# A gate ahead of GpSimd's first load, a re-planned order, and a last tile of 384 and 128 columns

## The chip, the core and the metric

The kernel runs on one core of a Trainium2 chip. Its engines have queues of their own: TensorE (PE, with PEld for weight loads), VectorE (DVE), ScalarE (ACT), GpSimd (POOL) and SyncE (SP, which here only issues DMAs). The metric is the time of one execution in device microseconds: 287.45 us, the median of three runs (285.32 to 287.76).

## What is computed

A linear attention over 8 batches, 8 heads, 576 tokens and 64 channels, and an FFN with a maximum over three products:

```python
def phi(x):
    proj = np.einsum('bhsd,df->bhsf', x, w_phi)
    proj = proj - np.max(np.abs(proj), axis=-1, keepdims=True)
    return np.concatenate([np.exp(proj), np.exp(-proj)], axis=-1)
...
kv = np.einsum('bhsf,bhsd->bhfd', phi(k), v)
num = np.einsum('bhsf,bhfd->bhsd', phi(q), kv)
den = np.einsum('bhsf,bhf->bhs', phi(q), z)[..., None] + 1e-06
...
h = np.maximum(np.maximum(x @ w1, x @ w2), x @ w3)
return h @ w_out
```

z is the sum of phi(k) over the tokens; x is num / den with the heads of a token side by side (4608 x 512); w1 to w3 are 512 x 768, w_out is 768 x 512.

## The kernel before

The attention is cut into 16 units of four heads (two units a batch), the FFN into nine chunks of 512 tokens: eight of 512 of a batch's 576 tokens, and a last one of the eight batches' remaining 64.

A unit goes through these steps. Its q, k and v are loaded. q and k become bf16 (qk_bf) and are turned by PE (tps) or by a DMA transpose into qkT. PE projects them (psq, psk). DVE takes the largest absolute values (mqp for q, mk for k), ACT makes the exponentials Ek of k. The maxima of k become a factor em, and GpSimd multiplies v with it into vab (line 589) and copies em beside it (line 599). PE projects q a second time with the maxima taken off (psm), ACT makes Eq from it. PE multiplies Ek and vab into kv (kvps, line 643, 72 matmuls), then Eq and kv (psn), DVE divides, and the result is turned into xT.

How q and k come in differs by unit. Unit 0's q and k come in two halves each, four loads on SP's queue (line 447), and ACT casts them. Units 1 to 3 are loaded by GpSimd's queue with a cast on the way (line 458). Later units come as float32, and GpSimd casts them (line 476). v comes as float32 by SP or GpSimd (line 472). For some v loads a DVE copy of one element into the target (line 467) makes the load wait until some unit's qkT is there; this is called a gate.

The four weights come through GpSimd's queue (w_load, line 419): w1, w2 and w3 into w_bf, w_out into wout_bf. h is computed as x w1 + max(0, x (w2 - w1), x (w3 - w1)), so GpSimd subtracts w1 from the second and third weight (line 785), three pieces each, before the FFN's first products (ups, line 714), and a product w1 w_out is made once: w1 is turned by PE (pwT) and multiplied (pm, line 811). A chunk's output tile is xT times this product (ops, line 742) plus the maximum times w_out (line 747); it is copied to SBUF (line 755) and stored (line 762).

The order of all this is written out by hand: PLAN lists every step as number, engine, buffers and a start time, and plan() hands the steps to their engines in this order. The start times aren't waited for on the chip; what waits is each engine, in its own order, for the data and buffers of its next instruction. DVE's queue begins with memsets and three casts of w_phi (lines 405 and 406), whose two halves ACT's queue loads. fill() puts matmuls of constants (idlers, line 842) where PLAN leaves PE a gap.

The last output tile is made in two pieces of 256 columns, so that the first piece's copy and store lie beside the second piece's matmuls.

Of the kernel before, what the change touches and what calls it, by code (L numbers as in the profile page):

```python
# [95 lines left out]
0G@0.7 4A@0.7 6S0@0.7 2D0@0.8 3D@1.0 10S0@1.2 1G@1.3 12S@1.6 85G0@1.9 8S@2.1 84G@2.6 1075G@3.3 158G1@4.0 5D@4.1  # L96
157G@4.7 7A2@5.0 14G0@5.5 1078G@6.2 11A@6.3 1076G@6.9 15T1@7.2 13A@7.3 361G1@7.7 16D0@7.8 360G1@8.4 21T002300@8.6
26T45@8.8 24D@9.0 9A@9.1 29D@9.6 28A@9.7 19T6@10.0 17T7@10.2 27A@10.2 20D@10.4 22A@10.7 227G2@10.7 41T1@10.7 18D@10.8
23A@11.1 226G@11.4 30D@11.4 31T24@11.5 36T67@11.8 32A@12.0 34D@12.0 90T5@12.1 33A@12.4 39D@12.6 88T2@12.7 38A@12.9
44D@13.2 37A@13.4 89D1@13.5 54T60@13.9 43A@13.9 40D@14.1 92T2@14.4 55A@14.5 86D1@14.7 93D@14.8 63T7@14.9 87S@14.9  # L100
25D@15.0 56A@15.0 114T11211@15.3 947S2@15.3 42A@15.5 35D@15.6 60T6@15.6 64A@15.7 1085T3@16.1 91D@16.2 65A@16.2
99T40@16.6 62A@16.7 45D@16.8 57T7@17.0 117D@17.1 61A@17.2 1089T5@17.4 159D3@17.4 102D@17.5 59A@17.6 104T16@17.9
1090D0@18.1 58A@18.1 163T4@18.3 46A0@18.6 118D@18.7 94T75@18.8 50A@18.9 164D2@19.0 115A@19.2 53G0@19.3 47G@19.5
116A@19.5 1086D@19.6 95A@19.7 165T4@19.8 66T2@20.0 96A@20.2 107D@20.2 48G@20.6 67A@20.7 166D@20.8 68A@21.0 109T31@21.0
97D@21.0 100A@21.2 1087T4@21.3 112D@21.6 51G@21.7 101A@21.7 161T2@21.8 106A@22.2 1088D@22.2 139T71@22.6 49A@22.7
52G@22.8 105A@22.8 130T3@22.8 98D@22.8 127T4@23.2 141A@23.3 103D@23.4 140A@23.5 131A@23.8 160G@23.9 69T057@24.0
162D@24.0 119A1@24.3 111A@24.5 120G1@24.7 129A@25.0 228D0@25.4 108D@25.4 121G@25.8 133T0@26.1 71D@26.2 70A@26.2
# [12 lines left out]
1111T0@45.7 257A@45.8 249D@45.9 1082G@45.9 201A@46.1 250D@46.5 258A@46.6 261T5@46.8 253A@46.9 202T2@46.9 262D1@47.1  # L120
366T004700@47.2 1112D@47.2 264A1@47.3 263S@47.3 214T056@47.5 1110A@47.6 369D@47.8 1083G@48.0 204A@48.1 229S@48.2
203A@48.6 381T01@48.6 426S1@48.6 216D@48.8 1123T4@48.9 248A@49.0 215D@49.2 384D@49.5 368A@49.5 211T2@49.8 386T6@49.9
385D@50.1 213A@50.1 299G1@50.1 1115T5@50.1 212A@50.4 367A@50.6 1124D@50.7 1107T0@51.0 382A@51.1 267G1@51.2 389D@51.3
556S0@51.3 298G@51.4 247A@51.6 370D@51.6 268T21@51.9 208T4@52.1 1108D@52.2 270A@52.3 1119T3@52.3 300S2@52.6 269A@52.7
1116D@52.8 1121T7@53.2 388A@53.2 265G@53.3 387A@53.5 209A@53.8 390D@53.9 371T02@54.1 210A@54.2 1120D@54.2 277T5@54.4
1117T6@54.6 383A@54.7 374D@54.8 278A@55.2 266G@55.3 1122D@55.4 280T4@55.5 271T3@55.6 279A@55.7 223T10@55.8 1118D@56.0
281A@56.1 274T0@56.1 555S0@56.2 1113T7@56.4 282A@56.4 224D0@56.6 273A@56.7 362S3@56.7 276A@57.2 376T56@57.3 559G2@57.4
283T141@57.6 272A@57.6 379D@57.7 275A@58.1 375D@58.3 428G0@58.5 391T3@58.8 1125T5@58.8 1114D@58.9 392A0@59.0 377A@59.2
393S@59.3 284D@59.5 429G@59.6 378A@59.6 1129T0@59.7 285D@59.9 491S0@60.1 373A@60.1 380D@60.3 372A@60.6 306T113711@60.7
430S1@60.8 316T41@60.9 310D@61.1 321T6@61.2 317A@61.3 221T2@61.4 309D@61.7 1130T@61.7 323A@61.8 319D@62.3 325D@62.9  # L130
219T3@63.0 320D@63.2 1131A0@63.2 217T4@63.3 1126T@63.6 394A0@63.7 222D1@63.8 318A@64.0 396G0@64.1 220D0@64.4 307A@64.4
# [160 lines left out]
def kernel(  # L292
# [133 lines left out]
    def attention(u):  # L426
# [4 lines left out]
        def nd(kind, *args, **kw):  # L431
            return node(kind, u, *args, **kw)
# [441 lines left out]
```

## Time and profile before

| | |
|---|---|
| median of three runs | 287.45 us |
| the profiled execution | 286.68 us |
| its span, from the first to the last instruction | 284.9 us |
| PE / DVE / ACT / POOL busy | 273.7 / 207.9 / 192.4 / 124.4 us |
| granted TensorE clock, mean | 0.998 |
| read from HBM / written | 34.67 / 9.44 MB |

The page's shares are averages over the span. The head (about the first 40 us) brings in the weights and the first units, the middle mixes units and FFN chunks, and the tail is FFN alone. In timelines a row gives start, length, engine, line, operation and tile; a bracket tells how long the engine stood idle ahead of it and what ended that. A DMA row on an engine is the issue alone; when its data land is told by the DMA view.

### The profile page before, as it was taken

What the parts mean: (1) busy time and instruction counts of PE and PEld (TensorE: products, weight loads), DVE (VectorE), ACT (ScalarE), POOL (GpSimd) and SP (SyncE); (2) the same over time, 40 slices, a digit from 0 to 9 for tenths busy, and PEclk for the clock granted to TensorE, in tenths of its full rate; (3) what the DMA queues carried; (4) which work ended last, traced back from release to release, by engine and by line L of the source; (5) the groups of instructions that cost most, each with busy time, mean ns of one, the idle gap of its engine ahead of it and who ended that gap; (6) DMA issues with size and microseconds to landing.
All of it is one profiled execution on the core that took longest, in us unless ns stands there. A gap on an engine that the chain in (4) does not pass through costs nothing.

```text
span 284.9 us, 8444 instructions
## 1 busy us (share of the span) xinstructions
PE 273.7 (96%) x3485; PEld 155.3 (55%) x3523; DVE 207.9 (73%) x442; ACT 192.4 (68%) x448; POOL 124.4 (44%) x104
## 2 busy tenths in 40 slices
PE   8789999989999999999999999999999999999995
PEld 3466674455665656556465565555544664444443
DVE  2799899989889886898678779987875462227431
ACT  3799779988899899967768887779775500041001
POOL 9359997786387543670554760160080601000000
PEclk9999999999999999999999999999999999999999
DMA  6999999999999979898995989293420035153126
GB/s 194 205 283 258 321 195 237 354 262 240 220 281 298 214 157 321 206 199 223 230 264 213 267 191 188 100 182 81 83 65 3 21 41 110 35 112 76 37 77 182
DMA packets 67760, 51.46 MB, mean 181 GB/s; under 512 B 48778, under 2 KB 53002, under 8 KB 67722
## 3 DMA queue, kind: packets, MB, share of 16 engines
q1 hardware_dynamic: 62761, 43.45, 62.6%
q0 software_dynamic: 4576, 7.28, 12.4%
q8 instruction: 27, 0.44, 0.6%
q10 hardware_dynamic: 385, 0.21, 0.3%
q14 instruction: 11, 0.09, 0.1%
HBM read 34.67 MB, written 9.44 MB: 155 GB/s over the span
## 4 chain that ended last, share of the span: by engine, by line
PE 76%; DMA 9%; DVE 6%; ACT 4%; issue 2%; POOL 1%; SPq 1%; ACTq 0%; POOLq 0%
PE ups L714 28%; PE ops L747 15%; PE ops L742 10%; PE psn L661 6%; PE kvps L643 6%; PE psm L614 4%; PE psq L535 4%; DMA q_raw<-in_q_dram 3%; ACT Ek L548 2%; DMA qkT<-mT 2%; DMA v_raw<-in_v_dram 2%; DVE mqp L554 2%; DMA xT<-x_sb 2%; DVE mk L554 2%; DVE hT L720 1%
## 5 line engine op out<-in xcount | busy, mean ns | idle before, releaser
L714 PE MATMUL ups<-xT,w_bf 128*128 128x512 bf16 x415 | 102.7, 379 | 1.0
L627 ACT ACTIVATE Eq<-psm 128x512 bf16<-128x512 f32 (+1 forms) x160 | 80.8, 591 | 10.9 <-PE psm L614 8.3
L589 POOL TENSOR_TENSOR vab<-v_raw,em 128x1152 bf16<-128x1152 f32 (+1 forms) x36 | 68.0, 1905 | 41.1 <-ACT em L585 23.8
L548 ACT ACTIVATE Ek<-psk 128x512 bf16<-128x512 f32 x128 | 72.2, 617 | 5.2 <-PE psk L535 4.1
L714 PEld LDWEIGHTS <-w_bf 128*128 128x128 bf16 x432 | 40.5, 98 | 44.6 <-issue 0.4
L720 DVE TENSOR_TENSOR hT<-hT,ups 128x512 bf16<-128x512 bf16 x54 | 36.4, 682 | 23.4 <-ACT hT L722 13.9
L554 DVE TENSOR_REDUCE mqp<-psq 128x4 bf16<-128x512 f32 (+1 forms) x80 | 48.8, 631 | 5.5 <-PE psk L535 2.8
L747 PE MATMUL ops<-wout_bf,hT 128*128 128x512 bf16 (+1 forms) x215 | 51.3, 373 | 0.4
L554 DVE TENSOR_REDUCE mk<-psk 128x4 f32<-128x512 f32 x64 | 43.0, 681 | 2.7 <-ACT Ek L548 1.7
L747 PEld LDWEIGHTS <-hT 128*128 128x128 bf16 x222 | 21.3, 98 | 23.2
L722 ACT ACTIVATE hT<-ups 128x512 bf16<-128x512 f32 x31 | 18.6, 617 | 21.4 <-PE ups L714 21.3
L668 DVE TENSOR_TENSOR x_sb<-psn,rden 128x320 bf16<-128x320 f32 x64 | 31.4, 491 | 2.2
L755 ACT COPY osb<-ops 128x512 f32<-128x512 f32 (+1 forms) x18 | 10.3, 586 | 31.9 <-PE ops L747 24.2
L661 PEld LDWEIGHTS <-Eq 128*128 128x128 bf16 x640 | 24.9, 97 | 7.7 <-ACT Eq L627 0.3
L755 DVE COPY osb<-ops 128x512 f32<-128x512 f32 x19 | 12.9, 687 | 19.3 <-PE ops L747 17.7
L661 PE MATMUL psn<-kv_sb,Eq 128*128 128x65 bf16 x640 | 26.6, 194 | 0.1
L742 PE MATMUL ops<-xT 128*128 128x512 bf16 x86 | 24.0, 379 | 0.5
L614 PE MATMUL psm<-qkT,wphi_m 128*128 128x512 bf16 (+1 forms) x70 | 22.3, 359 | 0.3 <-DMA qkT<-mT 0.3
L535 PE MATMUL psq<-w,qkT 64*128 64x128 bf16 x256 | 21.7, 217 | 0.8 <-PE psm L619 0.4
L643 PE MATMUL kvps<-vab,Ek 64*128 64x65 bf16 x1152 | 20.7, 190 | 1.3 <-POOL vab L589 0.7
L535 PE MATMUL psk<-w,qkT 64*128 64x128 bf16 x256 | 21.5, 217 | 0.4 <-DVE mqp L554 0.4
L535 PEld LDWEIGHTS <-qkT 64*128 64x128 bf16 x512 | 14.9, 94 | 11.7 <-issue 9.3
(76 smaller groups left out, 262.8 us busy)
## 6 DMA issues: line engine op xcount, KB each, us to landing
out_dram<-osb SPq DMA_DIRECT2D x65, 128.0 KB, 2.8
v_raw<-in_v_dram SPq DMA_DIRECT2D x14, 576.0 KB, 5.3
k_raw<-in_k_dram SPq DMA_DIRECT2D x11, 576.0 KB, 6.4
q_raw<-in_q_dram SPq DMA_DIRECT2D x11, 576.0 KB, 5.3
w_bf<-in_moe_w_dram POOLq DMA_DIRECT2D x3, 768.0 KB, 11.4
v_raw<-in_v_dram POOLq DMA_DIRECT2D x2, 576.0 KB, 14.2
qk_bf<-in_k_dram POOLq DMA_DIRECT2D x3, 288.0 KB, 12.0
qk_bf<-in_q_dram POOLq DMA_DIRECT2D x3, 288.0 KB, 12.9
```

The lines of the kernel that those rows point to most:

```text
L535: nc.tensor.matmul(ps()[:, i, :], lhsT=cols[r, :], rhs=w2[r, c, :], start=True, stop=True)
L548: nc.scalar.activation(Ek[s]()[:, tiles_of(t0, n), :], of(1), EXP, scale=1.0 - 2.0 * s)
L554: nc.vector.tensor_reduce((mq, mk)[c]()[:, tiles_of(t0, n)], of(c), AXX, ALU.max, apply_absolute_value=True)
L589: (nc.vector if n_.eng == "DVE" else nc.gpsimd).tensor_tensor(vab()[:, g, t0:t1, 0:D], vb()[:, t0:t1, :], em()[:, g, t0:t1].unsqueeze(2).t ...
L614: nc.tensor.matmul(psm()[:, 0:w], lhsT=wphi_m, rhs=rhs, start=True, stop=True)
L627: nc.scalar.activation(Eqb()[s][:, cols], psm()[:, 0:w], EXP, scale=1.0 - 2.0 * s)
L643: nc.tensor.matmul(kvps[ab]()[:, t // NT, g, :], lhsT=Ek[g]()[r, t, :], rhs=vab()[r, g, t, :], start=(t + g == 0), stop=(t == UT - 1 and g ...
L661: nc.tensor.matmul(psn()[:, c, :], lhsT=Eqb()[g][:, t0:t0 + P], rhs=kv()[:, pr, ab, g, :], start=(g == 0), stop=(g == 1))
L714: nc.tensor.matmul(ups(), lhsT=w_bf[i + 1][:, ct, j * P:(j + 1) * P], rhs=tokens_of(ct), start=(ct == 0), stop=(ct == CT - 1))
L720: nc.vector.tensor_tensor(hT()[:, j, :], hT()[:, j, :], ups(), ALU.max)
L742: nc.tensor.matmul(ops_()[:, 0:width], lhsT=tile_of(ct, tt), rhs=line_w[c_i > MOVE][:, ct, cols], start=(ct == 0), stop=False)
L747: nc.tensor.matmul(ops_()[:, 0:width], lhsT=hT()[:, j, tt * P:(tt + 1) * P], rhs=wout_bf[:, j, cols], start=False, stop=(j == JT - 1))
```

## The change

Three things change, the third by a new table alone.

First, GpSimd's loads of unit 1's q and k depend on a new DVE copy (a gate): it reads one element of each of two column blocks in the first half of unit 0's k and writes them into the buffer that the loads then fill. The loads are the first in GpSimd's queue, so what stands behind them waits as well.

Second, the last output tile is cut into 384 and 128 columns.

Third, PLAN is replaced as a whole. In its start numbers the last steps stand 1.7 us earlier, and the FFN's first product at 40.1 and no longer at 41.4. The third weight's load moves ahead of GpSimd's first vab. The number of idlers falls from 29 to 21.

```diff
 PLAN = """
-0G@0.7 4A@0.7 6S0@0.7 2D0@0.8 3D@1.0 10S0@1.2 1G@1.3 12S@1.6 85G0@1.9 8S@2.1 84G@2.6 1075G@3.3 158G1@4.0 5D@4.1
...
+0G@0.7 4A@0.7 6S0@0.7 2D0@0.8 3D@1.0 10S0@1.2 1G@1.3 12S@1.6 8S@2.1 7A0@3.6 5D@4.1 84D1@4.4 11A@4.4 86G@4.6 13A@5.2
...
+                        un[what, i] = n_
...
+                    need = []
+                    if u == 1 and what == 0:
+                        src = raw_bufs(0)[1]
+                        need = [nd("gate", {"DVE": 0.1}, lambda src=src: nc.vector.tensor_copy(
+                            qk()[0:1, :, 0, 0:1], src()[0:1, 0:2, 0:1]), [units[0][1, 0]], [src, qk])]
+                    elif u == 1:
+                        need = [gate]
+                    gate = need[0] if need else None
+
                     def main(what=what, ts=ts, p0=p0, p1=p1):
                         nc.gpsimd.dma_start(by_pairs(qk()[:, what, ts, :]), rows_of(what, u, p0, p1))
-                    cast[what, i] = cast[what, 1] = nd("L0" if u + i == 0 and u < HALVES else "L", {"POOL": 0.85}, main, [], [qk],
+                    cast[what, i] = cast[what, 1] = nd("L0" if u + i == 0 and u < HALVES else "L", {"POOL": 0.85}, main, need, [qk],
...
             halves = 2 if c_i == B and tt == SM // P - 1 else 1
-            width = DM // halves
+            widths = [DM] if halves == 1 else [DM - P, P]
             osb = buf("osb", OSB, [P, DM], FP32) if halves == 1 else None
-            for i in range(halves):
+            for i, width in enumerate(widths):
                 ops_ = bank("ops", [P, DM])
-                cols = slice(i * width, (i + 1) * width)
+                cols = slice(i * (DM - P), i * (DM - P) + width)
```

The lines behind the edits are numbered 10 higher after the change. In DVE's queue of the new kernel the gate (L461) stands behind the three casts of w_phi and ahead of the first copy of unit 0's qkT. In brackets stands what an instruction waits for; DMAHW is a DMA of SP or ACT.

```order
L405 CAST w2_73<-wphi_f_66 64x128 [waits DMAHW0_49]
L405 CAST w2_73<-wphi_f_66 64x128 [waits DMAHW2_49]
L406 CAST wphi_m_74<-wphi_f_66 64x128
L461 CAST qk_bf_129<-k_raw_105 1x2 [waits DMAHW3_49]
L506 COPY qkT_154<-tps_139 128x1024 [waits PE_49]
```

Before, the copy of qkT followed the third cast.

GpSimd's queue before, from its eighth load on, to the first vab; DMASW0 to DMASW7 are the landings of GpSimd's own DMAs, whose numbers come round after eight:

```order
L419 DMA w1_bf_82<-in_moe_w2_dram 128x4x768
L472 DMA k_raw_169<-in_k_dram 128x2x576 [waits DMASW0_49]
L472 DMA q_raw_179<-in_q_dram 128x2x576 [waits DMASW1_49]
L458 DMA qk_bf_226<-in_k_dram 128x2x576 [waits DMASW2_49,PE_49,Activation_49]
L458 DMA qk_bf_226<-in_q_dram 128x2x576 [waits DMASW3_49]
L599 CAST vab_456<-em_435 128x2x9 [waits Activation_49]
L589 TENSOR_TENSOR vab_456<-v_raw_142,em_435 128x9x64 [waits DMASW5_49]
L589 TENSOR_TENSOR vab_456<-v_raw_142,em_435 128x9x64 x3
L472 DMA v_raw_401<-in_v_dram 128x2x576 [waits DMASW4_49,DVE_49]
```

The same stretch of the new kernel:

```order
L419 DMA w1_bf_82<-in_moe_w2_dram 128x4x768
L482 DMA q_raw_241<-in_q_dram 128x2x576 [waits DMASW0_49]
L468 DMA qk_bf_265<-in_k_dram 128x2x576 [waits DMASW1_49,PE_49,Activation_49]
L482 DMA k_raw_287<-in_k_dram 128x2x576 [waits DMASW2_49]
L468 DMA qk_bf_265<-in_q_dram 128x2x576 [waits DMASW3_49]
L482 DMA v_raw_362<-in_v_dram 128x2x576 [waits DMASW4_49,DVE_49]
L419 DMA w2_bf_83<-in_moe_w3_dram 128x4x768 [waits DMASW5_49]
L609 CAST vab_454<-em_448 128x2x9 [waits Activation_49]
L599 TENSOR_TENSOR vab_454<-v_raw_184,em_448 128x9x64 x2
```

A v load (unit 2's) and the third weight have come between the twelfth load and vab. The six loads at the queue's start are the same in both, in another order: unit 1's k and q, w1, unit 2's k and q and unit 0's v before; unit 1's k and q, w1, unit 2's q, unit 0's v and unit 2's k after. On PE the transposes of unit 2, which need the sixth load, now stand ahead of and between four of unit 1's psm products, and unit 0's kv follows these.

The last matmuls on PE are those of the last tile's two pieces; the piece that is made first is the 128 columns, and the 384 columns come last, copied and stored by ACT.

296 lines of the change are left out of this document (148 added, 148 removed).

## The prediction

> **What bounds the kernel now.** I read the page first, then the busy time by stretches, then the timelines of single engines, then the landings of the DMAs. TensorE (PE) is busy almost throughout:
>
> ```profile
> PE 273.7 (96%) x3485; PEld 155.3 (55%) x3523; DVE 207.9 (73%) x442; ACT 192.4 (68%) x448; POOL 124.4 (44%) x104
> ```
>
> By stretches of 5 us (columns: stretch, its length, then busy time of PE, PEld, DVE, ACT, POOL, the granted clock, DMA) the head looks otherwise; the last row groups the idlers (count, duration in ns, first and last start):
>
> ```profile
> 20.00:25.00 5.00, 4.44 (x121) 3.42 (x120) 4.91 (x11) 5.00 (x16) 4.87 (x6) 1.00 1.14 287
> 40.00:45.00 5.00, 4.76 (x63) 2.82 (x58) 5.00 (x12) 4.13 (x8) 3.50 (x3) 1.00 1.21 153
> 45.00:50.00 5.00, 4.75 (x106) 2.80 (x108) 4.28 (x8) 4.45 (x13) 5.00 (x3) 1.00 1.05 304
> 55.00:60.00 5.00, 4.26 (x62) 2.28 (x63) 4.39 (x9) 5.00 (x12) 4.56 (x3) 1.00 1.17 251
> ...
> L842 PE MATMUL idler<-idle x29: 376/379/631, 1.0 to 38.5; 128*128 128x512 bf16 x29
> ```
>
> Until 38.5 us PE's busy time holds idler matmuls that compute nothing; in the head ACT, DVE and GpSimd (POOL) are as full as PE (20 to 25) and, with the DMAs, set the pace. Behind the first FFN matmul PE has next to no idle time, so each microsecond by which that point moves goes into the end. The question is when unit 0's kv product and, after it, that matmul start:
>
> ```profile
> 23.18 0.38 PE L616 MATMUL psm<-qkT,w 128*128 128x512 bf16 x1
> 23.74 0.19 PE L643 MATMUL kvps<-vab,Ek 64*128 64x65 bf16 x1
> 24.10 1.25 PE L643 MATMUL kvps<-vab,Ek 64*128 64x65 bf16 x71 [0.17 <-ACT Eq L627]
> ...
> 42.06 1.24 PE L714 MATMUL ups<-xT,w_bf 128*128 128x512 bf16 x4
> ```
>
> The kv product needs vab, which GpSimd makes in its own queue:
>
> ```profile
> 1.89 0.94 POOL L458 DMA_DIRECT2D qk_bf<-in_k_dram  x1
> 2.83 0.73 POOL L458 DMA_DIRECT2D qk_bf<-in_q_dram  x1
> 3.54 0.78 POOL L419 DMA_DIRECT2D w_bf<-in_moe_w_dram  x1
> ...
> 10.00 0.72 POOL L472 DMA_DIRECT2D k_raw<-in_k_dram  x1 [1.94 <-DMA qk_bf<-in_k_dram]
> 11.44 0.73 POOL L472 DMA_DIRECT2D q_raw<-in_q_dram  x1 [0.72 <-DMA qk_bf<-in_q_dram]
> ...
> 16.62 0.72 POOL L458 DMA_DIRECT2D qk_bf<-in_q_dram  x1 [0.40 <-DMA qk_bf<-in_k_dram]
> 19.16 0.26 POOL L599 CAST vab<-em 128x18 bf16<-128x18 f32 x1 [1.83 <-ACT em L585]
> 19.39 4.48 POOL L589 TENSOR_TENSOR vab<-v_raw,em 128x576 bf16<-128x576 f32 x4
> ```
>
> GpSimd's first six loads (unit 1's k and q, the first weight, unit 2's k and q, unit 0's v) land, by the DMA view of each issue (last column: us from issue to landing), so:
>
> ```profile
> qk_bf<-in_k_dram POOLq DMA_DIRECT2D x1, 288.0 KB, 7.8
> qk_bf<-in_q_dram POOLq DMA_DIRECT2D x1, 288.0 KB, 8.3
> ...
> qk_bf<-in_k_dram POOLq DMA_DIRECT2D x1, 288.0 KB, 12.0
> qk_bf<-in_q_dram POOLq DMA_DIRECT2D x1, 288.0 KB, 12.9
> v_raw<-in_v_dram POOLq DMA_DIRECT2D x1, 576.0 KB, 13.6
> ```
>
> With issues at 1.89 and 2.83 the first two land at 9.7 and 11.1; the others follow 0.7 to 0.8 us apart (4.3, 5.0, 5.7) and land at 16.3, 17.9 and 19.3. The ninth GpSimd DMA goes out at 10.00, the tenth at 11.44, the twelfth at 16.62: 0.3 us behind the landing of the first, second and fourth. GpSimd has eight DMA slots, and its n-th DMA holds the whole queue until the (n-8)-th has landed.
>
> **The gate.** The first load now waits for a one-partition DVE copy, which needs the first half of unit 0's k, but also stands behind three casts of w_phi in DVE's queue:
>
> ```profile
> 6.33 0.22 DVE L405 CAST w<-wphi_f 64x128 bf16<-64x128 f32 x1 [2.45 <-DMA wphi_f<-in_w_phi_dram]
> 6.57 0.22 DVE L406 CAST wphi_m<-wphi_f 64x128 bf16<-64x128 f32 x1
> 6.90 0.69 DVE L496 COPY qkT<-tps 128x1024 bf16<-128x1024 bf16 x1
> ...
> 14.84 0.13 DVE L467 CAST v_raw<-qkT 1x1 f32<-1x1 bf16 x1
> ```
>
> So the late landing is w_phi's second half, at 6.33. The copy takes the place at 6.90, costs 0.13 (row at 14.84), and GpSimd issues at about 7.05 and not at 1.89. What is queued behind it are all of GpSimd's loads; who waits are PE's transposes of units 1 and 2, the weights, and vab.
>
> How soon do packets flow after an issue? Queue 0 is GpSimd's, queue 1 SP's; the first line is 1.6 to 5.2 us, the next two 5.2 to 9.2, the last two 14 to 18.5 and 18.5 to 19:
>
> ```profile
> q1 hardware_dynamic: 437, 0.91, 76.9%
> ...
> q0 software_dynamic: 488, 0.54, 85.7%
> q1 hardware_dynamic: 139, 0.27, 21.5%
> ...
> q0 software_dynamic: 738, 1.20, 114.7%
> ...
> q1 hardware_dynamic: 34, 0.08, 44.7%
> ```
>
> Before 5.2 queue 0 has no row: nothing moves for 3.3 us from the issue at 1.89, while SP's loads fill the engines. The same is seen the other way round: SP issues a v load at 15.00 (below), and up to 18.5 only queue 0 has a row.
>
> ```profile
> 0.72 0.40 SPq L447 DMA_DIRECT2D q_raw<-in_q_dram  x1
> 15.00 14.81 SPq L472 DMA_DIRECT2D v_raw<-in_v_dram  x3
> ...
> DMA packets 0, 0.00 MB, mean 0 GB/s; under 512 B 0, under 2 KB 0, under 8 KB 0
> ```
>
> On empty engines SP's first load, issued at 0.72, has no packet before 1.7 (the last row, for 0 to 1.7) and flows then: 1.0 us. With the gate SP's four halves are nearly through when GpSimd issues (0.27 MB are left at 5.2, at 0.91 MB in 3.6 us another 1.1 us), so I am nearer to the empty case: the issue's own 0.94 us and 1.0, first packets at 9.0 (ends 8.05 and 10.35). The Trainium skill (DMA: Bandwidth & Descriptors, Specifications) gives about 1 us to the first byte on GpSimd's path; this case's only clean row says 3.3. By the rule the packets would flow at 8.05 and the sum below would be 0.95 us lower.
>
> **The six loads and the third weight.** From the first packet (5.2) to the sixth landing (19.3) were 14.1 us; 21.5% of 4.0 us, 0.9, of it went to SP's halves, which are now out of the way: 13.2, so 22.2 us. Unit 1's v, on SP, falls into this stretch; alone such a load takes 1.4 us (19.3 less 17.9), and it starts late behind a filled queue: 0 to 1.4, I take 0.7: 22.9. The order within the six changes, not their bytes.
>
> The third weight was issued behind vab, when its slot had long been free. Now it is GpSimd's fourteenth DMA, ahead of vab: it waits for the sixth landing, 0.3 us more, and issues for 0.78 (row at 3.54): 24.0. Then the cast (0.23 to the next start) and vab at 24.2, against 19.39; vab's 4.48 us end at 28.7, against 23.9. That it lands early is hidden: the subtraction that needs it is far from PE's path then, 0 us gained. PE's transposes of unit 2 also wait for the sixth load, but are done, with the four products behind them (0.56 each, the row at 23.18), before 28.7.
>
> **From the kv product to the FFN.** Before:
>
> ```profile
> 23.74:42.06 18.32, 17.21 (x387) 12.56 (x388) 16.61 (x40) 14.86 (x40) 17.55 (x15) 1.00 1.07 256
> ```
>
> 18.2 us from 23.9 to 42.06, PE busy for 17.2. The new order puts about 1.0 us of this ahead of kv (two products like the one at 23.18, 0.56 each, and a projection, less a small product that moves behind). PE's idle time here, 1.1 us, mostly waited for work that now has 4.8 us more time. Ends 17.3 and, if the stretch's last idlers also go, 15.6; I take 16.2, where PE has no idle time left. The first FFN matmul starts at 44.9: +2.8.
>
> **Behind it.** PE's idle time at 40 to 50 and 55 to 60 (0.24, 0.25, 0.74: 1.2 us) belongs to loads that are now issued earlier (unit 3's v ahead of 30 us) and to a row of maxima whose DMA stood behind GpSimd's queue. I take 1.0 as gone (ends 0 and 1.2). The fewer idlers cost nothing while PE waits anyway.
>
> **The tail.** The queue now ends with the 384 columns, not with the 128:
>
> ```profile
> 281.79 0.37 ACT L755 COPY osb<-ops 128x256 f32<-128x256 f32 x1 [0.76 <-PE ops L747]
> 282.19 0.35 ACTq L762 DMA_DIRECT2D out_dram<-osb  x1
> L755 ACT COPY osb<-ops 128x512 f32<-128x512 f32 (+1 forms) x18 | 10.3, 586 | 31.9 <-PE ops L747 24.2
> ```
>
> 256 columns are copied in 0.37 us, 512 in about 0.6: 384 in some 0.48, 0.1 more, and the last store has half as many bytes again (0 to 0.2). The matmuls stream 512 columns in all as before. I take +0.1.
>
> **Sum.** +2.8 - 1.0 + 0.1 = +1.9. The profiled execution took 286.7 us (span 284.9): 288.6. The median of the runs stands 0.8 above it: **289.4 us**, 0.7% slower. 1% (2.9 us) is about what a measurement of this kernel can tell from no change, so this would read as no change.
>
> **Rivals.** First, the gate opens early. If w_phi's second half comes with the k half, the gate opens at about 5.0: the cast of k starts at
>
> ```profile
> 4.60 0.67 ACT L451 CAST qk_bf<-k_raw 128x576 bf16<-128x576 f32 x1 [0.45 <-DMA k_raw<-in_k_dram]
> ```
>
> and the DVE copies need 0.4. Everything up to the FFN is 2.0 earlier: +0.8 - 0.9, 287.4. For it: w_phi's first half lands 2.9 us after its issue, so the second is late for some reason that may go away; against it: GpSimd's packets only start at 5.2, and SP's stay. The Trainium skill (the same page, Latency and other measured facts) names such a reason: two of the 16 engines are usually slower, as a best guess through the fetching of GpSimd's descriptors. No view here tells the engines apart. Chance 0.22.
>
> Second, the packets flow late. If the 3.3 us belong to GpSimd's first DMA itself, they start at 10.35 (+1.35), and v takes its full 1.4 (+0.7): the sixth load lands at 25.0, the FFN starts at 47.0, the end is 291.5, 1.4% slower. This one mechanism decides from a sixth landing at about 23.9 on, where 1% is reached. For it: it is the only row of a first GpSimd DMA. Against it: SP's late packets at 15.00 show the same delay on a queue that was not new, so it is the filled engines. Chance 0.22.
>
> Third, the plan holds: the table's own start numbers put the FFN 1.3 us earlier than before. With 1.0 behind it and 0.1 in the tail that is 285.3. The six loads would have to land by about 18, with first packets before 5: against the gate's own rows. Chance 0.05.
>
> **How the numbers follow.** Forecast 0.51. Its own spread, 288 to 291, leaves 0.14 of it over 290.3. The second rival gives 0.19 to slower and 0.03 to the same, the first all to the same but 0.01, the third 0.03 to faster and 0.02 to the same. Faster 0.04, same 0.63, slower 0.33. The range runs from the first rival less what a quicker first packet is worth (286.4) to the second with some of PE's idle time left (292.0).
>
> **What would show it.** Right: GpSimd's first load at about 7, released by DVE; its fourteenth DMA waiting for unit 2's k until about 23; vab at 24, kv at 29, the first FFN matmul at 45; less PE idle time at 45 to 60. Wrong: vab before 20; the fourteenth DMA without a wait; a gate that opens near 5; or PE finding other work before kv, so that the FFN moves by less.

## The result, and the profile after

The changed kernel takes **292.01 us** (median of six runs, 290.6 to 292.51), the kernel before beside it 287.61 us: a ratio of 1.0158 (95% interval 1.0123 to 1.0193), 1.6% slower. Predicted were 289.4 us, with 286.4 to 292.0 as the range: the time lies 0.01 us above its end, and the likeliest case (no change that can be told) didn't come. The profiled execution took 290.6 us (span 288.8), the fastest of the six. A few executions of the experiments were slow against the others of their kernel; medians and ratios leave them out, and a kernel whose profile is such a run has a dash in the table below.

The page's first line of the changed kernel, to be read beside the one of before, says nearly the same, since a share of busy time hides where PE waits:

```profile
PE 273.5 (95%) x3477; PEld 154.8 (54%) x3515; DVE 207.5 (72%) x440; ACT 193.1 (67%) x446; POOL 125.5 (43%) x109
```

The stretches say more. First the changed kernel (columns as above: busy time of PE, PEld, DVE, ACT, POOL, granted clock, DMA share, GB/s):

```profile
5.00:10.00 5.00, 4.08 (x57) 2.50 (x57) 3.33 (x8) 2.67 (x5) 3.45 (x5) 1.00 0.47 98
10.00:15.00 5.00, 3.11 (x54) 1.80 (x52) 3.51 (x8) 3.52 (x9) 4.15 (x6) 1.00 1.09 156
20.00:25.00 5.00, 2.93 (x48) 1.88 (x47) 3.69 (x8) 3.60 (x13) 2.19 (x5) 0.98 1.17 262
25.00:30.00 5.00, 4.59 (x98) 3.51 (x98) 3.83 (x8) 3.60 (x11) 4.33 (x5) 0.68 1.18 224
40.00:45.00 5.00, 4.95 (x111) 3.91 (x112) 4.46 (x14) 4.03 (x11) 5.00 (x4) 1.00 0.64 135
45.00:50.00 5.00, 4.91 (x42) 2.44 (x38) 5.00 (x10) 5.00 (x12) 5.00 (x5) 1.00 0.92 184
55.00:60.00 5.00, 5.00 (x48) 2.62 (x45) 4.97 (x11) 5.00 (x14) 4.24 (x5) 1.00 1.18 322
65.00:70.00 5.00, 3.60 (x64) 2.24 (x57) 2.96 (x8) 3.04 (x8) 2.12 (x1) 1.00 1.18 261
```

and three stretches of the kernel before that the prediction didn't show:

```profile
5.00:10.00 5.00, 3.73 (x37) 1.72 (x34) 2.42 (x5) 1.47 (x3) 3.06 (x6) 1.00 1.08 204
10.00:15.00 5.00, 4.45 (x76) 3.04 (x77) 4.38 (x10) 4.97 (x12) 1.44 (x2) 1.00 1.17 208
65.00:70.00 5.00, 4.89 (x74) 3.31 (x75) 4.59 (x16) 4.66 (x14) 3.36 (x3) 1.00 1.13 225
```

Four things are to be seen. At 5 to 10 us the DMA engines are half idle (share 0.47, 98 GB/s, against 1.08 and 204). At 10 to 25 PE waits more than before. At 40 to 60 its waits have gone, as predicted (4.95, 4.91 and 5.00, against 4.76, 4.75 and 4.26). At 65 to 70 there is a new one: 3.60 against 4.89.

GpSimd's queue in the changed kernel, the rows that answer to those of before (start, length, engine, line, operation; in the bracket the idle time ahead and what ended it):

```profile
6.55 0.94 POOL L468 DMA_DIRECT2D qk_bf<-in_k_dram  x1 [4.61 <-DVE qk_bf L461]
...
18.24 0.73 POOL L482 DMA_DIRECT2D k_raw<-in_k_dram  x1 [4.10 <-DMA w_bf<-in_moe_w_dram]
...
23.89 0.76 POOL L419 DMA_DIRECT2D w_bf<-in_moe_w_dram  x1 [1.81 <-DMA qk_bf<-in_k_dram]
24.65 0.28 POOL L609 CAST vab<-em 128x18 bf16<-128x18 f32 x1
24.82 4.49 POOL L599 TENSOR_TENSOR vab<-v_raw,em 128x576 bf16<-128x576 f32 x4
```

The first load waits for DVE's copy until 6.55. The third weight's load waits 1.81 us for unit 2's k, the sixth of the queue's first loads, and vab follows at 24.82 (before 19.39). On PE:

```profile
23.65 0.63 PE L503 MATMUL tps<-ident,qk_bf 128*64 128x128 bf16 x15 [1.64 <-DMA qk_bf<-in_k_dram]
29.36 1.27 PE L653 MATMUL kvps<-vab,Ek 64*128 64x65 bf16 x72 [0.41 <-POOL vab L599]
45.53 1.89 PE L724 MATMUL ups<-xT,w_bf 128*128 128x512 bf16 x7
68.86 0.39 PE L624 MATMUL psm<-qkT,wphi_m 128*128 128x512 bf16 x1 [1.24 <-DMA qkT<-mT]
```

Unit 0's kv product starts at 29.4 (before 23.7), the first FFN matmul at 45.53 (before 42.06): 3.47 us later. The last row is the new wait: unit 5's psm waits for mT, the row of maxima that a small DMA (4.5 KB) writes into qkT. From the first FFN matmul to the end of PE's work it is 239.84 us, and was 239.65. From there to the end of the span it is 3.45 us, and was 3.18. Together: 3.47 + 0.19 + 0.27 = 3.9 us of span.

### The profile page after: what moved, and what is told of

Read it like the earlier page. It is cut to its first block, busy times and chain, and to the rows that moved or that the text cites. A ratio compares the mean times of both kernels' runs of the same rounds, so it can differ in the third digit from the quotient of the medians.

```text
span 288.8 us, 8435 instructions
## 1 busy us (share of the span) xinstructions
PE 273.5 (95%) x3477; PEld 154.8 (54%) x3515; DVE 207.5 (72%) x440; ACT 193.1 (67%) x446; POOL 125.5 (43%) x109
## 4 chain that ended last, share of the span: by engine, by line
PE 75%; DMA 9%; ACT 6%; POOL 3%; DVE 3%; issue 2%; ACTq 1%
PE ups L724 27%; PE ops L757 15%; PE ops L752 10%; PE psn L671 6%; PE kvps L653 5%; DMA qk_bf<-in_k_dram 5%; PE psm L624 5%; PE psq L545 4%; DMA qkT<-mT 3%; ACT Ek L558 3%; ACT Eq L637 2%; POOL vab L599 2%; DMA wphi_f<-in_w_phi_dram 2%; PE pm L821 1%; DVE mk L564 1%
## 5 line engine op out<-in xcount | busy, mean ns | idle before, releaser
L637 ACT ACTIVATE Eq<-psm 128x512 bf16<-128x512 f32 (+1 forms) x160 | 81.9, 583 | 16.4 <-PE psm L624 10.9
L558 ACT ACTIVATE Ek<-psk 128x512 bf16<-128x512 f32 x128 | 73.4, 624 | 10.8 <-PE psk L545 6.8
L757 PE MATMUL ops<-wout_bf,hT 128*128 128x512 bf16 (+2 forms) x216 | 51.5, 373 | 0.5 <-issue 0.3
L564 DVE TENSOR_REDUCE mk<-psk 128x4 f32<-128x512 f32 x64 | 43.1, 684 | 3.0 <-PE psk L545 1.8
L732 ACT ACTIVATE hT<-ups 128x512 bf16<-128x512 f32 x30 | 17.8, 606 | 20.7 <-PE ups L724 20.6
L765 ACT COPY osb<-ops 128x512 f32<-128x512 f32 (+2 forms) x19 | 10.8, 582 | 30.2 <-PE ops L757 12.7
L765 DVE COPY osb<-ops 128x512 f32<-128x512 f32 x18 | 12.2, 687 | 18.8 <-PE ops L757 17.2
L653 PE MATMUL kvps<-vab,Ek 64*128 64x65 bf16 x1152 | 20.0, 190 | 0.4 <-POOL vab L599 0.4
```

Source lines behind the costliest of these rows:

```text
L558: nc.scalar.activation(Ek[s]()[:, tiles_of(t0, n), :], of(1), EXP, scale=1.0 - 2.0 * s)
L564: nc.vector.tensor_reduce((mq, mk)[c]()[:, tiles_of(t0, n)], of(c), AXX, ALU.max, apply_absolute_value=True)
L637: nc.scalar.activation(Eqb()[s][:, cols], psm()[:, 0:w], EXP, scale=1.0 - 2.0 * s)
L653: nc.tensor.matmul(kvps[ab]()[:, t // NT, g, :], lhsT=Ek[g]()[r, t, :], rhs=vab()[r, g, t, :], start=(t + g == 0), stop=(t == UT - 1 and g ...
L757: nc.tensor.matmul(ops_()[:, 0:width], lhsT=hT()[:, j, tt * P:(tt + 1) * P], rhs=wout_bf[:, j, cols], start=False, stop=(j == JT - 1))
```

## The experiments

The kernels, grouped by what they start from. "FFN" is the start of the first FFN matmul, "behind" the time from there to PE's end. Both come from one profiled execution of each kernel, so a difference of a few tenths there says little. The ratio is to the kernel before on the same chip.

| run | what differs | median us | ratio to before [95%] | FFN | behind |
|---|---|---|---|---|---|
| before | | 286.9 to 287.6 | | 42.06 | 239.65 |
| b1 | before + gate | 292.46 | 1.0163 [1.0118, 1.0208] | 47.18 | 239.92 |
| f2 | before + gate, unit 1's v early | 290.30 | 1.0123 [1.0095, 1.0151] | 44.56 | 239.56 |
| e2 | before, unit 14's v later | 288.09 | 1.0040 [1.0009, 1.0071] | 40.98 | 240.10 |
| c3 | before, tail 384 + 128 | 288.01 | 1.0027 [1.0001, 1.0053] | 42.39 | 240.51 |
| after | | 292.01 | 1.0158 [1.0123, 1.0193] | 45.53 | 239.84 |
| a1 | after, no gate | 291.30 | 1.0138 [1.0105, 1.0170] | 44.34 | 243.00 |
| a2 | after, third weight late | 292.25 | 1.0165 [1.0114, 1.0215] | 45.09 | 242.52 |
| a3 | both of these | 290.04 | 1.0114 [1.0072, 1.0156] | 43.11 | 242.05 |
| c4 | a2 + six idlers | 292.15 | 1.0212 [1.0180, 1.0245] | 45.43 | 240.50 |
| c2 | after, gate ahead of w_phi | 290.98 | 1.0146 [1.0105, 1.0186] | - | - |
| e3 | after, unit 1's v early | 289.99 | 1.0105 [1.0070, 1.0141] | 45.62 | 239.04 |
| e1 | after, unit 14's v later | 289.90 | 1.0107 [1.0055, 1.0158] | - | - |
| e4 | a3, unit 14's v later, even tail | 288.87 | 1.0076 [1.0047, 1.0104] | - | - |
| f1 | after, four edits | 291.68 | 1.0161 [1.0133, 1.0189] | 44.37 | 241.09 |
| c1 | after, loads behind mT | 296.12 | 1.0358 [1.0311, 1.0405] | 45.32 | 248.75 |
| d1 | after, mT on ACT's queue | 299.22 | 1.0419 [1.0373, 1.0465] | 45.87 | 249.01 |
| d2 | a3, mT on ACT's queue | 296.89 | 1.0326 [1.0263, 1.0389] | 42.74 | 247.12 |
| d3 | d2, idlers, even tail | 293.31 | 1.0194 [1.0135, 1.0253] | 42.61 | 246.40 |

### The parts of the change, apart (a1, a2, a3, b1)

a1, the gate's copy writes elsewhere:

```diff
-                            qk()[0:1, :, 0, 0:1], src()[0:1, 0:2, 0:1]), [units[0][1, 0]], [src, qk])]
+                            gate_to[0:1, 0:2, 0:1], src()[0:1, 0:2, 0:1]), [units[0][1, 0]], [src, qk])]
```

> The changed kernel, but the gate's copy writes two elements that nobody reads, so GpSimd's loads wait for nothing (the copy itself stays in DVE's queue). Theory A (the loss is the late start of GpSimd's six loads, and the third weight's load ahead of vab, which waits for the sixth landing): loads go out at 1.9 and not 6.55, the sixth lands at about 20 and not 23.6, vab starts at 21.3 and not 24.8, the first FFN matmul at 42 and not 45.5; time 288.6 against 292.0. Theory B (the new order of PE's and the other queues is the loss, the gate is covered): the FFN stays at 45, time above 291. Theory C (the granted clock, which fell to 0.68 at 25 to 30 us): the dip stays, since PE waits as before, and the time falls by under 1.

a2, the third weight's place in PLAN (a3 has both edits):

```diff
-1078G@15.6
+1078G@36.9
```

> The changed kernel with the gate, but the third weight's load stands behind vab again, where the kernel before had it. Theory A with vab as the only gate of the kv product: vab starts at 22.4 and not 24.8, kv at 27.0 and not 29.4; time 289.7. Theory A with a second gate close behind (PE's transposes of unit 2, which wait for the sixth load, and the four psm products behind them at a granted clock of 0.68, done at 28.3): kv at 28.4, time 291.0. Theory B: no change, 292.

> Both: no wait for the gate and the third weight behind vab; what stays of the change is the new order and the last tile of 384 and 128. Theory A: sixth landing 20, vab at 19 to 20, kv at 24.4 (PE's transposes of unit 2 and the products behind them), first FFN matmul 40.6; time 287.2, at or under the kernel before (287.6). Theory B: 290 or more.

b1, in the kernel before; GpSimd's loads are then written behind the copy, in the same order:

```diff
         nc.vector.tensor_copy(wphi_m[0:D, :], wphi_f[0:D, :])
+        nc.vector.tensor_copy(units[1]["qk"]()[0:1, :, 0, 0:1], raw_bufs(0)[1]()[0:1, 0:2, 0:1])
```

> The kernel before with nothing but the gate (the copy behind the casts of w_phi, GpSimd's first load waits for it; order, third weight and last tile as before). Theory A: GpSimd's first load at 6.6, sixth landing (unit 0's v) 23.3, vab 23.4 and not 19.4, kv at 28.0 and not 23.9, the first FFN matmul at 45.2 with up to 1.1 us of PE's idle time filled; time 290.6, if the waits behind the first FFN matmul stay, 289.6 if they go. Theory B: 287.6 to 288.2.

Neither theory holds alone. The gate by itself costs the old order 1.6% (theory A's 290.6 was too low). The order with the last tile, without the gate and with the third weight late, costs 1.1% (A said level). Both together cost 1.6%, not 2.7%: they don't add. The third weight's place costs nothing that can be told (a2 against after). In a2 vab starts 2.2 us sooner, the kv product only 0.5:

```profile
22.62 4.47 POOL L599 TENSOR_TENSOR vab<-v_raw,em 128x576 bf16<-128x576 f32 x4
...
28.88 1.30 PE L653 MATMUL kvps<-vab,Ek 64*128 64x65 bf16 x72
```

GpSimd's row for vab in a3 shows one reason why the order is slower without the gate, too:

```profile
21.91 0.26 POOL L610 CAST vab<-em 128x18 bf16<-128x18 f32 x1 [3.23 <-ACT em L596]
```

GpSimd had waited 3.2 us for em, whose ACT operation began at 21.4 (before 18.59); the loads were there. By the first FFN matmul 1.05 us of it are left (43.11 against 42.06). The larger part of a3's loss, 2.4 us, lies behind that point (242.05 against 239.65). The whole of b1's loss, in contrast, stands ahead of the first FFN matmul (5.1 us later). There GpSimd has em, and vab's first product waits for unit 0's v, the sixth load in that order:

```profile
21.77 0.26 POOL L601 CAST vab<-em 128x18 bf16<-128x18 f32 x1 [0.99 <-ACT em L587]
24.90 4.49 POOL L591 TENSOR_TENSOR vab<-v_raw,em 128x576 bf16<-128x576 f32 x4 [2.87 <-DMA v_raw<-in_v_dram]
```

Given the gate, the new order shortens the way from the kv product to the FFN, as the prediction said: it takes 16.2 us, in b1 17.2 (30.02 to 47.18).

The last column holds the second finding. In the order of before, "behind" is 239.6 to 240.5 in all five kernels, wherever the FFN starts between 41.0 and 47.2. In the new order it is 239.8 to 243.0 in the first four, and an earlier start of the FFN doesn't bring an earlier end: 43.1 ends at 285.2, 44.3 at 287.3, 45.5 at 285.4. So it isn't PE's own work alone that sets the pace there: it waits for something. PE's waits for mT behind the FFN's start (total, times, longest) in the kernel before, the changed kernel and a1:

```profile
PE psm L614 <- DMA qkT<-mT: 0.3, 1, 0.3
...
PE psm L624 <- DMA qkT<-mT: 1.5, 2, 1.2
...
PE psm L625 <- DMA qkT<-mT: 3.0, 2, 2.3
```

In a2 and a3 they are 3.0 as well. Less these waits, "behind" is 238.3 in the changed kernel (239.5 in a2, 239.1 in a3) and 239.4 in the kernel before (239.1 to 240.3 in the other four of its order): up to 1 us of what the prediction counted on is there, and the waits for mT take it back. In a1 a reduced clock comes on top: 0.66 at 70 to 75 us, behind the wait.

### The wait for mT (c1, d1, d2, d3)

c1, the loads of two units behind mT on SP's queue:

```diff
-491S0@54.3 492S0@54.8 686S1@78.0 622S1@78.5
+491S0@58.1 492S0@58.2 686S1@83.3 622S1@83.4
```

> The changed kernel, but on SP's queue the rows of maxima (mT) of units 5 and 6 are sent ahead of the two loads of raw q and k that stood ahead of each. After four runs the theory is in two parts: A1, the gate moves the kv product and with it the first FFN matmul; A2, behind the first FFN matmul the new order loses what its removed waits gave, because mT stands behind two loads of 576 KB each and PE's psm waits for it (1.5 us in the profiled execution of the changed kernel, 3.0 in each of the three kernels with the new order tried so far, 0.3 in the kernel before). By A2 the waits of psm for mT go, first FFN matmul to the end of PE's work takes 238.3 to 239 us and not 239.8 to 243, time 289.5 to 290.5. Rival: the moved loads make the casts of units 7 and 9 late and PE waits for those: 291.5 or more.

The rival held, and worse than it said: 296.1. The wait at 65 to 70 did go (psm at 67.29, nothing waited for), and a longer one came at 82, for xT, whose transposes stood on SP behind a transpose that waited for the late loads' casts:

```profile
67.29 0.38 PE L624 MATMUL psm<-qkT,wphi_m 128*128 128x512 bf16 x1
...
82.28 2.29 PE L724 MATMUL ups<-xT,w_bf 128*128 128x512 bf16 x5 [3.73 <-DMA xT<-x_sb]
```

d1, mT of units 3, 5 and 6 by ACT:

```diff
-264S@45.9 394S@58.0 459S@83.2
+264A@45.9 394A@58.0 459A@83.2
```

> The changed kernel, but the rows of maxima (mT) of units 3, 5 and 6 are sent by ACT's queue and not by SP's; no load moves. The run that moved the loads behind them showed PE busy through 60 to 75 us and then a new wait of 3.7 us at 82 for xT, whose transposes stood behind unit 7's late casts. If mT is late because it stands behind SP's two loads (A2), it lands 2 to 3 us after its issue now, psm's waits for mT go (1.5 in the profile of the changed kernel), and nothing behind is delayed: time 289.5 to 290.5. If all DMA engines are full there and a small transfer is late on any queue: 292, with the waits as they were. If the chain of loads, casts and transposes sets the pace at 60 to 95 anyway, the wait comes back at another place: 291.5 to 292.

> No gate, the third weight behind vab (the third run: 290.0, with 3.0 us of waits for mT behind the first FFN matmul) and mT of units 3, 5 and 6 on ACT's queue. If those waits are the order's whole loss behind the FFN's start: 287.2 to 287.8, level with the kernel before. If they come back elsewhere: 289 to 290.

> As the run just named, and six more idlers on PE ahead of unit 0's second transposes, where PE waited 1.7 us in that order and the granted clock then fell to 0.66 at 10 to 15 us, and the last tile in two pieces of 256 again. If the dip delays unit 0's maxima (em at 21.4, against 18.6 in the kernel before): clock 1.00, em at 20, the first FFN matmul at 41.8 and not 43.1, time 286, at or under the kernel before. If the dip is covered: 287 to 288, 0.2 under the run just named for the tail alone.

d1 took 299.2: worse again. The first fence has the issue of unit 5's mT on SP in the changed kernel. In the second, from d1, the first row groups ACT's issues of mT (durations in ns, first and last start), then come the psm that waits and PE's waits for mT:

```profile
63.52 0.78 SPq L580 DMA_DIRECT2D qkT<-mT  x1
```

```profile
L580 ACTq DMA_DIRECT2D qkT<-mT x2: 754/1034/1313, 51.7 to 65.1; - x2
...
72.25 0.39 PE L624 MATMUL psm<-qkT,wphi_m 128*128 128x512 bf16 x1 [2.86 <-DMA qkT<-mT]
...
PE psm L624 <- DMA qkT<-mT: 6.0, 3, 2.9
```

From issue to psm 5.3 us on SP's queue (63.52 to 68.86), 7.1 on ACT's (65.1 to 72.25): a queue of its own didn't help. In d1 SP, which no longer waits for mT, also sent three loads some 3 us earlier (the last at 50.33, not 53.28) and another at about 63, not 64.41: mT's wait had held loads back. The Trainium skill (DMA: Bandwidth & Descriptors, Queues, rings and completion order) says that the engines take turns between the queues' rows, packet by packet; by that the small transfer on a queue of its own should land sooner, and here it did not. d2 and d3 confirm d1 in the order without the gate (PE's waits for mT 5.6 and 4.9 us). The clock at 10 to 15 us, which had been 0.66 in a3, was 1.00 in d2 already, so that d3's idlers had nothing to keep up: its FFN starts 0.1 us earlier. The medians of d2 and d3 are 3.6 us apart, their profiled executions (295.12 and 294.0) only 1.1; what of it is the edits' own isn't told apart.

Why psm waits in the new order and hardly did before is in the rows of unit 5's mT and its first psm: before, then e3 (its own part follows), then a1:

```profile
61.41 0.77 SPq L570 DMA_DIRECT2D qkT<-mT  x1
67.06 0.70 PE L614 MATMUL psm<-qkT,wphi_m 128*128 128x256 bf16 x3
...
63.61 0.77 SPq L581 DMA_DIRECT2D qkT<-mT  x1
68.12 0.39 PE L625 MATMUL psm<-qkT,wphi_m 128*128 128x512 bf16 x1 [0.41 <-DMA qkT<-mT]
...
62.34 0.77 SPq L581 DMA_DIRECT2D qkT<-mT  x1
68.75 0.39 PE L625 MATMUL psm<-qkT,wphi_m 128*128 128x512 bf16 x1 [2.31 <-DMA qkT<-mT]
```

Before, mT had 5.7 us from its issue until psm was due, and PE didn't wait. In the new order it goes out 18.0 us behind the FFN's start, and psm is due at 22.1 (its start less its wait): 4.1 us, the same in the changed kernel, e3 and a1. From issue to psm it then took 4.5 us in e3, 5.3 in the changed kernel and 6.4 in a1, and PE waited for the rest: 0.41, 1.24 and 2.31. In c1, with the loads behind it, 4.0 were enough (63.31 to 67.29). So the transfer isn't slower than before; the new order leaves it less time.

### Bytes in the full stretch (e1 to e4)

By now the theory was that the DMA engines as a whole are full from 10 to 100 us. e1 and e2, unit 14's v; e3, unit 1's v, whose own gate then writes elsewhere:

```diff
-948S0@42.4
+948S0@126.0
...
-947S2@15.3
+947S2@42.5
...
-88S@14.6
+88S@2.6
```

> The changed kernel, but the load of unit 14's v (576 KB, SP, issued at 48.3; its data are wanted far later) goes out some 80 us later. Theory D, formed on the last runs: from 10 us to about 100 us the DMA engines are the bound (mean busy share 0.92 to 1.18 of the profile's measure in nearly every stretch), so that mT, transposes and loads only change places in a full queue, which is why the last two ideas made it worse; the gate leaves these engines half idle at 5 to 10 us (0.47 against 1.08, 98 GB/s against 204), and the new order at 40 to 50 (0.64 and 0.92 against 1.21 and 1.05, with unit 14's v moved from 15 us into the full stretch behind). By D this run has 576 KB less in front of PE's needs: waits for mT 0 to 0.5, time 290 to 290.6, 1.5 to 2 lower. Rival (a chain of waits, in which bytes don't count): 292.

> The kernel before with unit 14's v not at 15 us but where the changed kernel has it, ahead of unit 4's loads. Theory D: 576 KB more in the full stretch, PE waits for mT or for qkT of unit 4, 288 to 289. But the load also shared the engines with the kernel's first loads at 15 to 23 us; if that was what it cost, 286.5. Rival: 287.

> The changed kernel with the gate, but unit 1's v (576 KB) is issued by SP at 2.6, behind unit 0's four halves, and not at 16.5 (its own gate writes elements that nobody reads). Theory D: the idle engines of 5 to 10 us are used, and the load no longer shares with GpSimd's six: sixth landing at 22.2 and not 23.6, the first FFN matmul at 44.2, time 290.6. Rival: GpSimd's first packets wait behind this load as they did behind the halves in the kernel before: landings as before, 292.

> No gate, the third weight behind vab (290.0 in the third run), unit 14's v some 80 us later and the last tile in 256 and 256. Theory D: the waits behind the FFN's start (3.0) fall to 1, time 288; level with the kernel before at best, since em and the FFN stay 1 us later than there.

e1 (289.9, 1.0107) can't be told from the changed kernel: the two intervals overlap. e2 moved as the theory says, by 0.4%. e3 (290.0, 1.0105) stands where e1 does, with a narrower interval that still touches the changed kernel's. Its profiled execution is 0.7 us faster (289.9 against 290.6), and none of that lies ahead of the FFN, which starts no earlier: PE's clock was 0.81 and 0.85 at 25 to 35 us and took back what vab gained (23.35). The gain is behind: 239.04, with 0.6 us of waits for mT.

That the head gained by unit 1's v isn't shown either. The third weight's load, which waits for the sixth landing, goes out at 22.42 in e3 and at 23.89 in the changed kernel, but GpSimd's first load went out 0.5 us sooner too (6.03 and 6.55). From the one to the other it is 16.4 and 17.3 us; in c1 and d1, which don't touch the head, it is 16.3 (6.47 to 22.73) and 18.0 (6.29 to 24.24). e4 came to 0.8% slower than before, the nearest of the new order; against a3 (1.1%) it has the even tail as well, which by c3 accounts for about 0.3%.

### The gate's cost taken apart, and all together (f2, f1)

> The kernel before with the gate (292.5 in the fourth run), and unit 1's v issued by SP at 2.6 and not at 15. Theory D (the gate costs idle time of the DMA engines at 5 to 10 us, and the sixth load shares with unit 1's v): unit 0's v lands at 23.3 and not 24.8, vab and the first FFN matmul 1.5 earlier, 290.5 to 291. Rival (the gate costs by the place of GpSimd's queue alone): 292.5.

f2 is b1 with `87S@2.6` for `87S@14.9`; unit 1's v no longer waits for its own gate. The FFN starts at 44.56 and not 47.18, and the median is 2.2 us lower, though the intervals of the ratios overlap (1.0095 to 1.0151 and 1.0118 to 1.0208). GpSimd no longer waits for v:

```profile
22.35 0.26 POOL L602 CAST vab<-em 128x18 bf16<-128x18 f32 x1 [1.45 <-ACT em L588]
22.52 4.48 POOL L592 TENSOR_TENSOR vab<-v_raw,em 128x576 bf16<-128x576 f32 x4
```

By these two profiles half of the gate's 5.1 us in the old order (2.6 us) goes when unit 1's v no longer shares the engines with the six loads and comes in while they were half idle. The gate also opened 0.3 us sooner here (GpSimd's first load at 6.00, in b1 6.30), and one profile of each kernel doesn't tell how much of the rest is chance. The other half remains.

> The changed kernel with its gate and four edits that each moved work out of the way: unit 1's v at 2.6 (290.0 alone), unit 14's v some 80 us later (about 291 alone), the third weight behind vab (nothing alone) with four idlers ahead of unit 2's transposes, the last tile in 256 and 256 (0.3% the other way in the kernel before). Theory D, if the gains add: 290.0 less 0.7, less 0.8, less up to 1 for vab and the clock: 287.5 to 288.5, level with the kernel before, not faster. If they have the same cause and don't add: 289.5 to 290.

f1 has the edits of e3, e1 and a2, four idlers and the even tail. The gains don't add: 291.7, with 2.5 us of waits for mT again, though the FFN starts 1.2 us earlier than in the changed kernel. No kernel here beats the kernel before.

### Clock, gate, tail (c4, c2, c3)

```diff
+        if n.kind == "T" and n.u == 2 and n.costs["PE"] > 0.4 and ...
+            todo += [(n.start - 0.01, make(n.bufs[-1].index))] * 6
...
-84D1@4.4
+84D1@4.05
```

> The changed kernel with the third weight behind vab (as in the second run, where vab ended at 27.1 and kv only started at 28.9, PE's granted clock at 0.82 and 0.84 between 20 and 30 us), and six more idlers on PE ahead of unit 2's transposes, where PE waited 2.8 us. If the granted clock falls because PE sat idle, it stays near 1.00 in 20 to 30 us, kv starts at 27.3, the first FFN matmul at 43.5 and not 45.1, and the time is 1.5 under that run's 292.2. Rival: the idlers delay unit 2's transposes as much as the clock gains, or the clock falls all the same: 292.

Two stretches of a2, then of c4:

```profile
20.00:25.00 5.00, 2.02 (x26) 1.46 (x23) 2.14 (x6) 2.56 (x10) 3.70 (x6) 0.82 1.19 249
25.00:30.00 5.00, 5.00 (x136) 3.78 (x134) 4.50 (x9) 3.78 (x11) 2.19 (x3) 0.84 1.17 239
```

```profile
20.00:25.00 5.00, 4.28 (x43) 2.12 (x43) 2.96 (x6) 3.91 (x13) 3.90 (x6) 1.00 1.17 261
25.00:30.00 5.00, 4.26 (x125) 3.24 (x125) 4.98 (x9) 4.27 (x12) 2.87 (x3) 1.00 1.18 223
```

With the idlers the clock is 1.00, and no time is gained (1.0212 against a2's 1.0165; the intervals overlap). kv starts 0.5 us sooner (28.34), the FFN doesn't (45.43, in a2 45.09), so whatever the dip cost, it didn't reach the FFN.

> The changed kernel with the gate's copy ahead of the three casts of w_phi in DVE's queue, so that it waits for unit 0's k half alone. By A1: GpSimd's first load at about 5.2 and not 6.5, sixth landing 22.3 and not 23.6, the first FFN matmul 1.2 earlier, time 290.8. Rival (the packets then queue behind unit 0's second halves on SP, and those come later in turn): no gain, 292.

GpSimd's first load went out at 5.19, as expected, but the time (1.0146) can't be told from the changed kernel's. Whether the 1.4 us by which the gate opens sooner are worth the expected 1.2 stays undecided.

> The kernel before with the last tile cut into 384 and 128 columns and nothing else. The prediction's term: +0.1. Measured between the profiles of before and after: PE's end to the span's end 3.44 and not 3.19, +0.25. Time 287.3 to 287.9 against 287.3; the span behind PE's end 3.4. Rival: nothing, the store's fixed time hides the copy.

c3 is the tail's diff alone, in the kernel before: +0.3%. PE's end to the span's end is 3.45, and over all profiles 3.44 to 3.47 in every kernel that ends with 384 columns, 3.17 to 3.20 in every one that ends with 256. The last copy is the visible part of it (before: 0.37):

```profile
285.44 0.48 ACT L765 COPY osb<-ops 128x384 f32<-128x384 f32 x1 [1.40 <-PE ops L757]
```

## Why the prediction was wrong

**The gate: right.** It opens at 6.55 (7.05 predicted), released by DVE. The first packets flow 1.65 us behind the issue, at 8.2 (9.0), between the ends of 1.0 and 3.3. That refutes the second rival's mechanism: a first GpSimd DMA doesn't take 3.3 us by itself. The filled engines of before fit; no run tests them alone.

**The six loads: mis-sized.** From the first packet to the sixth landing it took 15.4 us (23.6 less 8.2), not 13.9. The first three loads took as long as before: the first weight landed 9.8 us behind the first packet (8.2 to 18.0), before 9.7 (5.2 to 14.9). The excess lies behind it, where SP issues unit 1's v at 16.47: 5.6 us to the sixth landing, before 4.4. That v would cost 0.7 was then too little; but in c1, with the same head, the sixth load was there some 1 us sooner, so part of it is this execution's. The earlier packets made up for half: sixth landing 23.6, not 22.9.

**The third weight and vab: the place right, the price not its own.** The load waited for the sixth landing and went out at 23.89 (24.0 predicted); vab started at 24.82 (24.2) and kv at 29.36 (28.7). But a2 put the load back, vab started at 22.62, and nothing was won: kv only came to 28.88, since PE's transposes of unit 2 wait for the same sixth load and the four products behind them ran at a reduced clock. The prediction had these done "before 28.7" and so off the path; they stood 0.5 us from it.

**kv to the FFN: the sum right, with luck.** 16.17 us against 16.2. But the prediction had PE busy for all of it:

```profile
29.36:45.53 16.17, 15.47 (x359) 11.45 (x362) 13.66 (x36) 13.23 (x33) 15.35 (x13) 1.00 0.93 245
```

1.7 us of work left the stretch (17.21 less 15.47), not 1.0, and 0.7 us of PE's idle time stayed where none was to. The two errors cancel. First FFN matmul 45.53 against 44.9.

**Behind it: the step that failed.** -1.0 was predicted, +0.2 measured. The waits at 40 to 60 went, as said. What was wrong is that they were counted as gained: a wait that goes is gained only if the next thing is ready, and no row was read for what is late next. It is mT: 1.5 us of waits (before 0.3), and 2.5 to 3.0 in a1, a2, a3 and f1. The new order has psm due 4.1 us behind mT's issue, before 5.7, and the transfer took 5.3. The prediction put this wait at nothing. The table's own start numbers held a warning: 1.7 us earlier at the end, 1.3 of them already ahead of the FFN, so 0.4 behind it, not 1.0.

**The tail: mis-sized.** +0.27 against +0.1.

**The median.** It stands 1.4 us above the profiled execution and not 0.8. With 0.6 (kv), 1.2 (behind), 0.2 (tail) and 0.6 (median) the 2.6 us between 289.4 and 292.0 are accounted for.

**The rivals.** The first put 287.4 on a gate that opens at 5.0; c2 opened it at 5.2 and took 291.0. w_phi's second half let DVE start its cast at 5.71 (before 6.33), still 2.1 us behind the first half's, though no GpSimd packet had moved yet: GpSimd's loads weren't the whole reason for its lateness. The third (the plan holds) fell with the FFN at 45.5.

What stays open is why mT takes 4.5 us from issue to psm in one kernel of the new order and 6.4 in another, and with it most of the spread from 239.0 to 243.0 us behind the FFN. That its place on SP's queue counts, but that neither another place nor another queue makes the kernel faster, is shown (c1, d1, d2). That full DMA engines are the reason fits the shares of 0.9 to 1.2 and e2, but e1 didn't settle it, and f1, with fewer bytes in the stretch, had the waits back. GpSimd's wait of 4.10 us for the first weight (to 18.24) needs no further cause: its load took as long from the first packet as before, only later.

## What to carry to other kernels

When a change removes waits in the middle of a kernel, name the next late thing before counting the gain, and look at whether the end has followed the start of that stretch at all. Ask also how much time each small transfer is left between its issue and its use, and whether the new order shortens it. A gate on a queue's first load also costs the time in which the transfer engines then stand idle; look for a load that waits for nothing and can fill it (here the medians fell by 2 us in both orders, though each time the intervals still touched). A small transfer that someone waits for can also be what holds back the big ones behind it; moving it to a free queue can make everything later.

## What the runs showed of the hardware

PE's granted clock can fall behind a stretch in which PE sat idle. In c1, whose unit 1 q came late, PE was busy for 1.89 of 5 us, and the next stretch ran at half clock:

```profile
10.00:15.00 5.00, 1.89 (x24) 1.16 (x24) 2.47 (x6) 3.04 (x7) 3.75 (x6) 0.83 1.07 151
15.00:20.00 5.00, 5.00 (x61) 3.27 (x58) 2.87 (x7) 3.00 (x7) 1.05 (x2) 0.50 1.14 265
```

In the changed kernel it was 0.68 behind 2.93 of 5 us. The Trainium skill (TensorE: Matmul & The Clock Gate, Part 1: The HAM clock gate) ties the clock to how busy PE has lately been; these traces agree.

Means over 5 us hide steps. In all 19 traces the clock is either 1.00 or 0.50, and 0.50 for 3.41 us or twice that (until the end cuts the last one off). In the changed kernel:

```profile
21.38:24.79 3.41, 1.55 (x29) 1.04 (x28) 2.10 (x5) 2.10 (x7) 1.60 (x3) 1.00 1.18 251
24.79:28.20 3.41, 3.41 (x45) 2.40 (x41) 2.71 (x5) 2.44 (x6) 3.41 (x5) 0.50 1.20 211
```

Cut into stretches of 3.41 us that fall in with these steps, the traces show where the limit lies (the first and last 3 us left out): each of the 19 stretches at full clock with at most 1.57 us of PE's busy time is followed by one at 0.50, and each one with 1.70 or more by one at 1.00. The three cases between go both ways (1.63 to full, two of 1.69 to half clock). So about half a stretch of work keeps the clock, and the same wait can cost it or not, by where the cuts fall. At 5 to 10 us PE was busy for 2.50 us in d2 and for 2.75 in a3, yet d2 kept its clock, with 2.18 and 1.96 us in its two stretches, and a3, with 1.57 in one, lost it. Idlers lift a stretch over the limit: a2's of 1.10 us (19.78 to 23.19) was followed by half clock, and c4, with idlers there, stayed at 1.00.

A 4.5 KB DMA took 4.5 to 6.4 us from issue to use on a queue with loads just ahead of it (e3, the changed kernel, a1), at most 4.0 with the loads behind it (c1), and 7.1 us on another engine's queue (d1).
